# A second DMA queue and a new work order for the first quarter of a local-attention and feed-forward kernel

## The chip, the cores and the metric

The kernel runs on one core of one Trainium2 chip. The metric is device time of one execution in microseconds, the median of several runs. Everything is float32 in memory; each product is made of three matmuls of float32 halves, as told below.

## What is computed

```python
def reference(A_x, A_wqkv, A_wo, B_w1, B_w2):        # x 1x2048x640, wqkv 640x1920, wo 640x640, w1 640x1536, w2 1536x640
    xn = layernorm(A_x)
    q, k, v = heads(xn @ A_wqkv)                     # 32 heads of 20
    logits = q . k at positions s, s-2, ..., s-14    # 8 positions, dilation 2, masked below 0
    s = (softmax(logits * 20 ** -0.5) . v) @ A_wo
    g = silu(silu(xn @ B_w1) @ B_w2)
    return A_x + s * g
```

## The kernel before

The 2048 tokens are four groups of 512, and a group is four tiles of 128 tokens. For each group the kernel makes qkv in four quarters of the heads (`qkv_phase`), then the output projection of the group before, then the feed-forward part. A weight is cut into units of 128 rows: a unit is loaded raw, ScalarE copies it to its high half (L410), VectorE or GpSimd subtracts to get the low half (L413), and TensorE multiplies high by high, low by high and high by low. The transposed activations are split in the same way into `th` (high) and `tl` (low).

The order of the work isn't written out. Each operation is recorded with an engine, an estimated duration, what it reads and writes, and a priority; `Weave.order` then plays the program through with its own estimates and lines up, for each engine, whatever can start first. TensorE's operations alone keep the order in which they are recorded. So a changed priority or estimate moves instructions on ScalarE, VectorE, GpSimd and SyncE (SP, which issues DMAs) as far as the plan reaches.

The change is about the first quarter of group 0 (`first_quarter`), in which nothing has been loaded yet:

- `warm` (L625) fills TensorE with 22 transposes of the identity, `WARM`, before the first real work, and 3 more, `WARM2`, after the transposes of tile 0. Their results aren't used.
- SP issues x of tile 0 in two halves (L685), then the weight units and x of tiles 1 to 3 (L439), in the order of their priorities (`X_AT` for the x tiles). A weight unit is two DMAs: its q columns (L376, 96 KB) and its k and v columns (L377, 160 KB). In this text w0 to w4 are the five units of the first quarter, and x0 to x3 the four tiles.
- `begin(t)` is tile t's layernorm: `bn_stats` (L639), `bn_aggr` (L640), a square root on ScalarE (L453), a reciprocal (L455) and the scaling (L644, in two parts for tile 0). `turn(t)` transposes the tile on TensorE (L654), copies the high half on ScalarE (L658) and subtracts the low half on VectorE (L662).
- `products` (L667) records the 60 matmuls of 128x512 (L676), 15 for each tile: tile by weight high, tile low by weight high, tile by weight low.
- The low halves of the first weights go to VectorE for the units in `ON_DVE`, to GpSimd for the others below `LO`.

Engines work their queues in order: an instruction that waits holds up all that stand behind it on its engine.

Of the kernel before, what the change touches and what calls it, by code (L numbers as in the profile page):

```python
# [14 lines left out]
P = 128  # L15
# [8 lines left out]
T = 4  # L24
# [7 lines left out]
WARM, WARM2 = 22, 3  # L32
# [7 lines left out]
X_AT = 2, 7, 8  # L40
TILE_AT = 1, 1.5, 2, 2.5
LOW_AT = 3
ON_DVE = (2, 3, 4)
# [18 lines left out]
class Weave:  # L62
# [11 lines left out]
    EARLY = 10.0, 0.6  # L74
# [63 lines left out]
    def order(self):  # L138
# [6 lines left out]
        lanes = {e: [0.0] * self.LANES for e in ("SP", "POOL")}  # L145
# [5 lines left out]
        while len(done) < len(self.ops):  # L151
# [31 lines left out]
            if o.nbytes:  # L183
                dma = max(dma, t + dur) + o.nbytes / self.RATE
# [28 lines left out]
def local_attention_silu_ffn(ctx: ExitStack, tc: tile.TileContext, x, wqkv, wo, w1, w2, out):  # L213
# [84 lines left out]
    def dma(fn, reads, writes, nbytes, prio, dur=0.45, late=0.0):  # L298
        add("SP", dur, fn, reads, writes, prio, nbytes=nbytes, late=late)
# [52 lines left out]
    def raw_load(k):  # L352
# [17 lines left out]
        if u[0] == "q":  # L370
# [3 lines left out]

            def go():
                nc.sync.dma_start(r[:, :w], all3[:, 0, q * BQ:q * BQ + w])  # L376
                nc.sync.dma_start(r[:, w:].rearrange("p (s m) -> p s m", s=2), all3[:, 1:, q * CQ:(q + 1) * CQ])  # L377
            dma(go, [], kr, n * P * 4, 1 + k if k < 2 * DC else clock[0] + 5, dur=0.9,
                late=0.2 * k if k < 2 * DC else 0.0)
# [9 lines left out]
    def w_load():  # L389
# [16 lines left out]
        if not k:  # L406
# [8 lines left out]
            due if pool_does else LOW_AT if k < LO else 50, lock=True)  # L415
# [22 lines left out]
    def load_x(g, t, n=1, prio=None):  # L438
        dma(lambda: nc.sync.dma_start(XIN[:, t:t + n], rows(xg, g)[:, t:t + n]), [],  # L439
            [("xin", u) for u in range(t, t + n)], n * P * D * 4, clock[0] if prio is None else prio,  # L440
            late=LATE if g else 0.4 * t)
# [179 lines left out]
    def first_quarter(i):  # L621
# [6 lines left out]
        pe(4.5, lambda: warm(WARM, ROT[0]), ["consts"], [("rot", 0)])  # L628
# [54 lines left out]
        for k in range(2):  # L683
            cs = slice(k * 320, (k + 1) * 320)
            dma(lambda cs=cs: nc.sync.dma_start(XIN[:, 0, cs], rows(xg, 0)[:, 0, cs]), [],  # L685
                [("xin", 0) if k else ("xin", 0, "a")], P * 320 * 4, 0)
# [13 lines left out]
        products(0, [(0, 0), (1, 0), (0, 1), (1, 1), (2, 0), (0, 2), (1, 2)])  # L700
        turn(1)
        products(0, [(2, 1), (0, 3), (1, 3), (2, 2)])
        products(1, [(0, 0), (0, 1), (0, 2)])
        products(0, [(0, 4), (1, 4)])
        products(1, [(0, 3), (0, 4)])
        products(0, [(2, 3), (2, 4)])
        products(1, passes(1, 2)[:-3])
        turn(2)
        products(1, passes(2)[-3:])
        products(2, passes(0, 1, 2)[:-3])  # L710
        turn(3)
        products(2, passes(2)[-3:])
        products(3, passes(0, 1, 2))
# [225 lines left out]
    act(1, lambda: nc.scalar.activation(SD[:, 1, 0:1], epst, AF.Sqrt), ["consts"], [("rs", 0)], 0, "sqrt")  # L939
# [39 lines left out]
```

## Time and profile before

| | us |
|---|---|
| median of 3 runs | 621.68 |
| the runs | 621.67 to 622.61 |
| the profiled execution, its own time | 621.44 |
| its span, first to last instruction | 619.7 |
| TensorE busy (matmul rows) | 614.2, 99% of the span |
| VectorE busy | 561.3, 91% |
| ScalarE busy | 309.5, 50% |
| GpSimd busy | 112.8, 18% |

The span is 1.74 us less than the execution's own time; that part lies around the instructions. In timelines the first number is the start in us from the span's start, the second the length, then engine, line, operation, what is written and read, and the count; a bracket tells how long the engine had been idle and who ended it. Matmuls overlap, so a row's length is more than its share of the pace: the pace is read from start to start. Rows with SPq are DMA issues.

### The profile page before, as it was taken

What the parts mean: (1) busy time and instruction counts of PE and PEld (TensorE: products, weight loads), DVE (VectorE), ACT (ScalarE), POOL (GpSimd) and SP (SyncE); (2) the same over time, 40 slices, a digit from 0 to 9 for tenths busy, and PEclk for the clock granted to TensorE, in tenths of its full rate; (3) what the DMA queues carried; (4) which work ended last, traced back from release to release, by engine and by line L of the source; (5) the groups of instructions that cost most, each with busy time, mean ns of one, the idle gap of its engine ahead of it and who ended that gap; (6) DMA issues with size and microseconds to landing.
All of it is one profiled execution on the core that took longest, in us unless ns stands there. A gap on an engine that the chain in (4) does not pass through costs nothing.

```text
span 619.7 us, 9092 instructions
## 1 busy us (share of the span) xinstructions
PE 614.2 (99%) x3357; PEld 555.3 (90%) x3357; DVE 561.3 (91%) x581; ACT 309.5 (50%) x651; POOL 112.8 (18%) x168
## 2 busy tenths in 40 slices
PE   8999999999999999999999999999999999999997
PEld 7889999998889999999888999999888999998997
DVE  6558999999989997999998999999979999899974
ACT  5435558937376213951944502583396316152750
POOL 4510000011101133111212233311121213311100
PEclk9999999999999999999999999999999999999999
DMA  8999999866999998764699999855579998956642
GB/s 248 343 287 324 354 345 391 356 236 186 304 322 348 328 356 259 238 195 139 203 242 251 340 333 304 276 176 163 169 202 278 251 334 277 316 179 202 206 124 103
DMA packets 65449, 162.45 MB, mean 262 GB/s; under 512 B 7053, under 2 KB 29165, under 8 KB 65405
## 3 DMA queue, kind: packets, MB, share of 16 engines
q0 software_dynamic: 20016, 82.58, 44.6%
q1 hardware_dynamic: 45389, 79.29, 40.6%
q8 instruction: 26, 0.43, 0.3%
q14 instruction: 18, 0.15, 0.1%
HBM read 109.55 MB, written 34.16 MB: 232 GB/s over the span
## 4 chain that ended last, share of the span: by engine, by line
PE 98%; SPq 1%; DMA 0%; DVE 0%; issue 0%
PE acc L766 22%; PE acc L768 15%; PE acc L737 10%; PE acc L739 10%; PE acc L738 10%; PE rot L883 9%; PE rot L884 9%; PE rot L882 9%; PE acc L676 2%; PE rot L768 1%; DMA pr<-in_A_wqkv_dram 0%; PE rot L766 0%; SPq L376 0%; PE acc L864 0%; SPq L377 0%; PE rot L654 0%
## 5 line engine op out<-in xcount | busy, mean ns | idle before, releaser
L739 PE MATMUL acc<-w,th 128*128 128x512 f32 (+1 forms) x300 | 112.4, 375 | 0.0
L738 PE MATMUL acc<-w,tl 128*128 128x512 f32 (+1 forms) x300 | 112.4, 375 | 0.0
L737 PE MATMUL acc<-w,th 128*128 128x512 f32 (+1 forms) x300 | 112.4, 375 | 0.0
L766 PE MATMUL acc<-w,sh 128*128 128x384 f32 x384 | 111.7, 334 | 0.0
L768 PE MATMUL acc<-w,sh 128*128 128x256 f32 x384 | 107.1, 279 | 0.0
L888 ACT ACTIVATE sh<-rot 128x512 fp32r<-128x512 f32 x48 | 28.6, 597 | 154.2 <-PE rot L884 154.2
L884 PE MATMUL rot<-th,w 128*128 128x512 f32 x240 | 93.8, 391 | 0.0
L883 PE MATMUL rot<-tl,w 128*128 128x512 f32 x240 | 93.8, 391 | 0.0
L882 PE MATMUL rot<-th,w 128*128 128x512 f32 x240 | 93.5, 389 | 0.0
L571 DVE TENSOR_TENSOR pr<-q,kv 128x2560 f32<-128x2560 f32 x32 | 90.2, 2819 | 1.2 <-DMA raw<-in_A_wqkv_dram 1.0
L609 DVE TENSOR_TENSOR pr<-e,kv 128x2560 f32<-128x2560 f32 x32 | 90.3, 2823 | 0.7
L574 DVE TENSOR_REDUCE l<-pr 128x128 f32<-128x2560 f32 x32 | 90.1, 2815 | 0.5
L614 DVE TENSOR_TENSOR pr<-pr 128x1280 f32<-128x1280 f32 x64 | 74.0, 1156 | 1.5
L402 POOL DMA_DIRECT2D w<-half_w x72 | 38.5, 534 | 190.1 <-PE acc L768 94.0
L766 PEld LDWEIGHTS acc<-w,sh 128*128 128x128 f32 x384 | 72.1, 188 | 1.1
L768 PEld LDWEIGHTS acc<-w,sh 128*128 128x128 f32 x384 | 72.2, 188 | 0.9
L402 POOL DMA_DIRECT2D w<-half_q x52 | 27.6, 531 | 238.8 <-PE rot L884 113.5
L737 PEld LDWEIGHTS acc<-w,th 128*128 128x128 f32 x300 | 56.3, 188 | 8.6
L739 PEld LDWEIGHTS acc<-w,th 128*128 128x128 f32 x300 | 56.3, 188 | 8.6
L738 PEld LDWEIGHTS acc<-w,tl 128*128 128x128 f32 x300 | 56.3, 188 | 8.6
L487 ACT ACTIVATE xin<-sf 32x256 f32<-32x256 f32 (+1 forms) x144 | 54.6, 379 | 9.7 <-DVE sf L514 8.0
L766 PE MATMUL acc<-w,sl 128*128 128x384 f32 x192 | 56.1, 332 | 0.0
(104 smaller groups left out, 1059.5 us busy)
## 6 DMA issues: line engine op xcount, KB each, us to landing
w<-half_w POOLq DMA_DIRECT2D x72, 640.0 KB, 6.1
w<-half_q POOLq DMA_DIRECT2D x39, 512.0 KB, 4.3
half_w<-w SPq DMA_DIRECT2D x24, 640.0 KB
w<-half_wo POOLq DMA_DIRECT2D x15, 640.0 KB, 5.6
kv<-kv SPq DMA_DIRECT2D x15, 560.0 KB
half_q<-w SPq DMA_DIRECT2D x15, 512.0 KB
kv<-kv SPq DMA_DIRECT2D x15, 420.0 KB
gate<-in_B_w_dram SPq DMA_DIRECT2D x16, 320.0 KB
```

The source lines that it names most:

```text
L571: dve(2560, lambda t=t: nc.vector.tensor_tensor(out=PR, in0=win(qq[:, t:t + 2, :], W, 0), in1=win(kv[:, 0, t:t + 2, :], W, CQ), op=OP.mult ...
L574: dve(2560, lambda t=t: nc.vector.tensor_reduce(out=l[:, t:t + 2].rearrange("p t w h -> p (t w h)"), in_=PR.rearrange("p t w (h d) -> p (t ...
L609: dve(2560, lambda t=t, v=v: nc.vector.tensor_tensor(out=PR.rearrange("p t w (h d) -> p t (w h) d", d=DH), in0=e[:, t:t + 2].rearrange("p ...
L614: dve(2 * k * CQ, lambda k=k: nc.vector.tensor_tensor(out=PR[:, :, 0:k, :], in0=PR[:, :, 0:k, :], in1=PR[:, :, k:2 * k, :], op=OP.add), [] ...
L737: nc.tensor.matmul(o, hi, wh, start=c == 0, stop=False)
L738: nc.tensor.matmul(o, lo, wh, start=False, stop=False)
L739: nc.tensor.matmul(o, hi, wl, start=False, stop=c == DC - 1)
L766: nc.tensor.matmul(a[t][0][:, :CA], st, w[:, :CA], start=first, stop=last)
L768: nc.tensor.matmul(b[t // 2][0][:, h * CB:(h + 1) * CB], st, w[:, CA:], start=first and h == 0, stop=last, skip_group_check=True)
L882: nc.tensor.matmul(h, wh[:, cs], TH[i][:, c, :], start=c == 0, stop=False)
L883: nc.tensor.matmul(h, wh[:, cs], TL[i][:, c, :], start=False, stop=False)
L884: nc.tensor.matmul(h, wl[:, cs], TH[i][:, c, :], start=False, stop=c == DC - 1)
```

## The change

It does the following in the first quarter.

- 18 dummy transposes in place of 22.
- The raw loads of units 1 and 3 (w1 and w3 below, `BY_ACT`) are issued by ScalarE's queue. They are recorded as reading a key that the first square root of 1 element writes, so the four issues stand behind the table load on ScalarE.
- Other priorities: `X_AT`, `TILE_AT` (layernorms) and `LOW_AT` (low halves, now one number for each unit), and another set `ON_DVE`.
- Another order of the 60 matmuls and the tiles' transposes on TensorE, as a string `FIRST`.
- Other constants in the planner's estimate of when early DMAs land.

```diff
-WARM, WARM2 = 22, 3
+WARM, WARM2 = 18, 3
-X_AT = 2, 7, 8
-TILE_AT = 1, 1.5, 2, 2.5
-LOW_AT = 3
-ON_DVE = (2, 3, 4)
+X_AT = 2, 4.5, 7
+BY_ACT = 1, 3
+TILE_AT = 1, 1.5, 2, 3
+LOW_AT = 1.2, 1.7, 1.9, 1.9, 2.6, 3
+ON_DVE = (1, 2, 3, 5, 6, 7)
+FIRST = """0h0 0x0 0h1 0x1 0w0 0h2 0x2 T1 0w1 0h3 0x3 1h012 0h4 0x4
+           1h34 0w2 0w34 1x01234 1w01 T2 1w234 2h01234 2x01234 2w01 T3 2w234 3h01234 3x01234 3w01234"""
...
-    EARLY = 10.0, 0.6
+    EARLY = 8.0, 0.1, 350e3
...
+            by, queue = ("ACT", nc.scalar) if k in BY_ACT else ("SP", nc.sync)
             def go():
-                nc.sync.dma_start(r[:, :w], all3[:, 0, q * BQ:q * BQ + w])
-                nc.sync.dma_start(r[:, w:].rearrange("p (s m) -> p s m", s=2), all3[:, 1:, q * CQ:(q + 1) * CQ])
+                queue.dma_start(r[:, :w], all3[:, 0, q * BQ:q * BQ + w])
+                queue.dma_start(r[:, w:].rearrange("p (s m) -> p s m", s=2), all3[:, 1:, q * CQ:(q + 1) * CQ])
...
-            due if pool_does else LOW_AT if k < LO else 50, lock=True)
+            due if pool_does else LOW_AT[min(k, DC)] if k < LO else 50, lock=True)
```

In `FIRST`, `0x2` is tile 0's low half by w2's high half, `h` is high by high, `w` high by low, and `T1` the transposes of tile 1. Line numbers of the changed kernel are a few higher than those before: L410 is L414, L453 is L457, L413 is L417, L376 and L377 are L381 and L382.

ScalarE, from the table load on (w_73 to w_77 are the high halves of w0 to w4, th is the activations' high half, the L453 rows are the square roots of the layernorms). Before:

```order
L939 ACT_TABLE_LOAD
L939 ACTIVATE sd<-epst 128x1
L453 ACTIVATE sd<-mv,epst 128x1
L410 ACTIVATE w_73<-pr 128x512
L658 ACTIVATE th_69<-rot_113 128x3x128
L658 ACTIVATE th_69<-rot_114 128x2x128
L410 ACTIVATE w_74<-pr 128x512
L453 ACTIVATE sd<-mv,epst 128x1
L410 ACTIVATE w_75<-pr 128x512
L410 ACTIVATE w_76<-pr 128x512
L658 ACTIVATE th_69<-rot_113 128x3x128
```

ScalarE in the changed kernel, from the four DMA issues on:

```order
L382 DMA pr<-in_A_wqkv_dram 128x2x160
L457 ACTIVATE sd<-mv,epst 128x1
L414 ACTIVATE w_73<-pr 128x512
L662 ACTIVATE th_69<-rot_113 128x3x128
L662 ACTIVATE th_69<-rot_114 128x2x128
L414 ACTIVATE w_75<-pr 128x512
L414 ACTIVATE w_74<-pr 128x512
L457 ACTIVATE sd<-mv,epst 128x1
L414 ACTIVATE w_76<-pr 128x512
L414 ACTIVATE w_77<-pr 128x512
L662 ACTIVATE th_69<-rot_113 128x3x128
```

The high half of w2 (w_75) now stands ahead of that of w1 (w_74), both stand ahead of tile 1's square root, and the high half of w4 (w_77) stands ahead of tile 1's th.

SP in the changed kernel, from x0 on, with the semaphores that an issue waits for (the eight DMAHW numbers are the completion semaphores of the DMAs issued before, given out in turn; pr of row 2 is w0, of rows 5 and 6 w2, of rows 8 and 9 w4):

```order
L689 DMA xin<-in_A_x_dram 128x320 x2
L381 DMA pr<-in_A_wqkv_dram 128x192
L382 DMA pr<-in_A_wqkv_dram 128x2x160
L443 DMA xin<-in_A_x_dram 128x640
L381 DMA pr<-in_A_wqkv_dram 128x192 [waits DMAHW0_49]
L382 DMA pr<-in_A_wqkv_dram 128x2x160 [waits DMAHW2_49]
L443 DMA xin<-in_A_x_dram 128x640 [waits DMAHW3_49]
L381 DMA pr<-in_A_wqkv_dram 128x192 [waits DMAHW4_49]
L382 DMA pr<-in_A_wqkv_dram 128x2x160 [waits DMAHW5_49]
L381 DMA raw<-in_A_wqkv_dram 128x192 [waits DMAHW6_49]
```

Before, SP's first seven DMAs after x0 waited for nothing and all ten weight DMAs were its own; now the two queues share the eight semaphores, w2's second part waits for w0's first part to land, and x2 for w0's second part.

TensorE in the changed kernel, the first matmuls (acc_107 is tile 0's bank, acc_108 tile 1's):

```order
L631 MATMUL rot_113<-ident 128x128 x18
L658 MATMUL rot_113<-ident,xin 128x128 x3
L658 MATMUL rot_114<-ident,xin 128x128 x2
L631 MATMUL acc_112<-ident 128x128 x3
L680 MATMUL acc_107<-w_73,th_69 128x512
L680 MATMUL acc_107<-w_73,tl_71 128x512
L680 MATMUL acc_107<-w_74,th_69 128x512
L680 MATMUL acc_107<-w_74,tl_71 128x512
L680 MATMUL acc_107<-w_73,th_69 128x512
L680 MATMUL acc_107<-w_75,th_69 128x512
L680 MATMUL acc_107<-w_75,tl_71 128x512
L658 MATMUL rot_113<-ident,xin 128x128 x3
```

The third matmul still takes w1's high half (w_74), as before; what changed ahead of tile 1's transposes is the number of dummies alone.

## Rows read from the trace of the kernel before

**Rows 1.** Busy time by windows, TensorE alone, from the second quarter to the end.
```profile
24.00:616.00 592.00, 592.00 (x3254) 1.00 0.86 262
```

**Rows 2.** The chain that ended last, its start: start us, us, what.
```profile
6.06 0.47 SPq L376
6.57 3.04 DMA pr<-in_A_wqkv_dram
9.64 0.74 PE acc L676 x2
```

**Rows 3.** The timeline of TensorE, 1 to 15 us.
```profile
5.27 1.06 PE L627 MATMUL rot<-ident 128*128 128x128 f32 x4
6.13 1.21 PE L654 MATMUL rot<-ident,xin 128*128 128x128 f32 x5
...
7.56 0.49 PE L676 MATMUL acc<-w,th 128*128 128x512 f32 x1
...
8.49 0.39 PE L676 MATMUL acc<-w,th 128*128 128x512 f32 x1
...
9.64 0.50 PE L676 MATMUL acc<-w,th 128*128 128x512 f32 x1 [0.31 <-DMA pr<-in_A_wqkv_dram]
...
10.22 0.71 PE L654 MATMUL rot<-ident,xin 128*128 128x128 f32 x5
...
13.76 1.30 PE L676 MATMUL acc<-w,tl 128*128 128x512 f32 x5
14.90 0.61 PE L676 MATMUL acc<-w,th 128*128 128x512 f32 x2
```

**Rows 4.** The timeline of ScalarE, 0 to 12 us.
```profile
2.04 0.20 ACT L939 ACTIVATE sd<-epst 128x1 f32<-128x1 f32 x1
4.35 0.30 ACT L453 ACTIVATE sd<-mv,epst 128x1 f32<-128x1 f32 x1 [2.10 <-DVE mv L640]
5.65 0.63 ACT L410 ACTIVATE w<-pr 128x512 fp32r<-128x512 f32 x1 [1.00 <-DMA pr<-in_A_wqkv_dram]
7.01 0.76 ACT L658 ACTIVATE th<-rot 128x384 fp32r<-128x384 f32 x2 [0.73 <-PE rot L654]
7.66 0.63 ACT L410 ACTIVATE w<-pr 128x512 fp32r<-128x512 f32 x1
8.77 0.29 ACT L453 ACTIVATE sd<-mv,epst 128x1 f32<-128x1 f32 x1 [0.48 <-DVE mv L640]
8.97 1.14 ACT L410 ACTIVATE w<-pr 128x512 fp32r<-128x512 f32 x2
```

**Rows 5.** The timeline of VectorE, 3 to 12 us.
```profile
3.08 0.99 DVE L639 BATCH_NORM_STATS2 st<-xin 128x6 f32<-128x320 f32 x2 [1.63 <-DMA xin<-in_A_x_dram]
...
4.88 0.80 DVE L644 TENSOR_SCALAR xin<-xin,mv,sd 128x384 f32<-128x384 f32 x2
6.41 0.49 DVE L639 BATCH_NORM_STATS2 st<-xin 128x6 f32<-128x320 f32 x1 [0.73 <-DMA xin<-in_A_x_dram]
7.54 0.56 DVE L662 TENSOR_TENSOR tl<-rot,th 128x384 fp32r<-128x384 f32 x1 [0.63 <-ACT th L658]
...
9.30 0.71 DVE L644 TENSOR_SCALAR xin<-xin,mv,sd 128x640 f32<-128x640 f32 x1
```

**Rows 6.** Busy time by windows: PE, PEld, DVE, ACT, POOL busy; PEclk, DMA share, GB/s.
```profile
3.00:4.50 1.50, 1.50 (x9) 1.50 (x8) 1.20 (x3) 0.15 (x1) 0.22 (x1) 1.00 0.61 159
4.50:5.65 1.15, 1.15 (x7) 1.15 (x6) 0.93 (x3) 0.15 (x2) 0.00 (x0) 1.00 0.99 356
7.66:9.64 1.98, 1.57 (x6) 0.79 (x5) 1.84 (x6) 1.50 (x5) 1.27 (x1) 1.00 0.92 250
0.00:6.41 6.41, 5.03 (x24) 5.03 (x25) 2.57 (x16) 2.41 (x4) 2.65 (x8) 1.00 0.59 188
0.00:7.66 7.66, 6.28 (x31) 6.15 (x31) 3.19 (x17) 3.06 (x6) 3.89 (x8) 1.00 0.65 200
```

**Rows 7.** The timeline of SP's DMA issues: that of w2's second part.
```profile
4.59 0.43 SPq L377 DMA_DIRECT2D pr<-in_A_wqkv_dram  x1
```

## What the change should do to the time

> **What bounds the kernel now.** I read the views in this order. First busy time by windows: from 24 us to 616 us TensorE is busy for 592.00 of 592.00 us [rows 1]. The reader is to see that nothing in that stretch can be gained or lost by moving other engines' work a little; only what TensorE does before it runs without a break counts. Second the chain that ended last: it leaves the DMA issues of SP at 6.57, goes through a transfer of a weight and reaches TensorE at 9.64; from there it is TensorE alone [rows 2]. Third TensorE's own timeline: real matmuls start at 7.56, in pieces with idle time between, and from 9.64 they follow each other [rows 3]. By 9.64 five of the 60 matmuls of the first quarter have been done: two start at 7.56 and 8.15 or so, three from 8.49. So the time is **the moment from which TensorE runs without a break, less what it has done by then**, plus a fixed rest. A matmul's pace is (14.90 - 13.76) / 5 = 0.23 us [rows 3].
>
> What ended the wait at 9.64? The row names a DMA, but ScalarE shows more: it starts two weight copies at 8.97, the first of them (w2's high half, half of 1.14 us) ends at 9.54, and TensorE takes it at 9.64. ScalarE had stood idle before, then run the square root of tile 1 at 8.77 [rows 4]. So w2 had landed by 8.97 at the latest, and ScalarE's order had a share in the delay.
>
> **The change part by part.**
>
> *Four dummies fewer.* The last four dummies begin at 5.27 and the transposes of tile 0 at 6.13 [rows 3]: the place comes free 0.86 us earlier. The scaling of tile 0 begins at 4.88 and its two parts take 0.80 us [rows 5], 384 columns ready by about 5.37, the rest at 5.68. So the transposes begin at about 5.4, some 0.7 us earlier, the casts to th at 6.3 in place of 7.01 [rows 4], and the first matmul at about 7.1 in place of 7.56. This is on the path only if what follows is ready too.
>
> *Tile 0's low half.* VectorE now has both bn_stats of tile 1 ahead of it, not one. Tile 1 landed at 6.41 and two bn_stats take 0.99 us, so 7.4, then 0.56 us for the subtraction [rows 5]: 7.96, against 8.10 before. Second matmul at 8.0.
>
> *Four issues on ScalarE.* ScalarE is free at 2.24 and has to take the square root of tile 0 at 4.35 [rows 4]. The trace has no DMA issue on ScalarE; the nearest row is SP's, 0.43 us [rows 7], so four end at about 4.0 and cost nothing. If one took more than 0.53 us the square root would come later; tile 0's first matmuls have 1.5 us to spare (below), so the bound above is still nothing on the path unless an issue takes 0.9 us.
>
> *When the weights land.* From 3.0 to 4.5 the DMA engines are busy for a share of 0.61 and move 159 GB/s, from 4.5 on for 0.99 [rows 6]. So earlier issues can recover at most what was idle: 0.39 x 1.5 = 0.59 us; ScalarE's first transfer, issued at 2.24 and with about a microsecond from issue to data as an estimate, can fill some 0.47 of it. What is behind it is the same bytes through full engines. Bytes also say how far a landing lags behind the moving: by 6.41 the engines had moved 188 x 6.41 = 1.21 MB, and tile 1 landed then, which with all issued ahead of it is 0.92 MB: a lag of 0.29 MB [rows 6]. In the changed kernel w1 and w3 run on one queue beside x1, w2 and x2 on the other. And the two queues share eight completion semaphores: SP may issue w2's second part only when w0's first part has landed, before 5.65 by the copy of w0 [rows 4], while it was issued at 4.59 before [rows 7]. So w2 no longer comes well ahead of w3: it lands when x0, w0, x1, w1, w2 (1.44 MB) and between none and all of w3 (to 1.70 MB) have. With the lag this is 1.73 to 1.99 MB moved. Before, 200 x 7.66 = 1.53 MB had been moved by 7.66, and 250 GB/s were moved after it [rows 6]: 8.46 to 9.50, less the 0.47 recovered: 8.0 to 9.0. I take **8.2**, near the early end, since the engines were not quite full in that stretch (0.92) and two queues leave them less idle.
>
> A rule speaks against this part. The Trainium skill ("DMA: Bandwidth & Descriptors", on issuing engines not being separate DMA queues) says that transfers issued by several engines run on the same 16 DMA engines and interleave, and that only the sequencer's issue time is saved. The trace's share of 0.99 from 4.5 us agrees; what the rule would make of the sum if issue time were all that counts is the fifth rival's mechanism below.
>
> *ScalarE's order.* This is the term that decides. The third matmul needs w1's high half, and ScalarE now makes w2's first. However early w1 lands, its copy waits for w2: 8.2, a copy of 0.63, a copy of 0.63 [rows 4], with 0.1 us for the hops: **w1's high half is ready at 9.55**, against a third matmul at 8.49 before [rows 3]. Behind it stands tile 1's square root: 0.29, then reciprocal and scaling (0.71 by its row [rows 5]), so tile 1 can be transposed some 1.25 us after w1's half. TensorE does five matmuls meanwhile, 5 x 0.23 = 1.15: level within 0.1 us. I add 0.05 for it. The low half of w1 on VectorE follows under the transposes (0.71 again for five of them [rows 3]).
>
> *The rest of the order* (low halves on VectorE in place of GpSimd, T2 and T3 one or two matmuls later) lies beside TensorE's unbroken run. I cost it at nothing; its cover is that weights 3 and 4 land before TensorE asks for them at about 11.7 and 13.0.
>
> **The sum.** TensorE runs without a break from 9.55 with two matmuls done, before from 9.64 with five: 9.55 - 9.64 + 3 x 0.23 + 0.05 = **+0.65 us**. With w2 at 8.0 or 9.0 it is +0.45 or +1.45. On the profiled execution's 621.44 this gives 622.1. The median of the runs shown is 621.68, 0.24 above that execution, so on it **622.3**. About 0.2% (1.24 us) is what a measurement can tell, so the forecast is no change, on the slow side.
>
> **The rivals.**
>
> 1. *The weights land early and the new flow works.* If w2 lands by 7.0 to 7.5 (the DMA engines gain from two queues more than the idle share says), w1's half is ready at 8.35 to 8.85: -0.55 to -0.05 with the same sum; if ScalarE has both even before th, TensorE could start its third matmul right at 8.2: -0.7. For it: the windows show idle DMA engines ahead of 4.5. Against: only 0.59 us of it. Time 621.0 to 621.6, I say 621.3.
>
> 2. *w4 becomes the wait, the slower side.* ScalarE's copy of w4 now stands ahead of tile 1's th, before it stood behind. TensorE asks for tile 1's th at about 12.1; the copy (0.63) and the first cast (0.4) must fit ahead of it, so w4 must land by 11.0. In the trace the copy of w4 comes later than 10.11, where w3's ends [rows 4], and x2 now runs ahead of w4. From 11.0 every microsecond adds one to the +0.65: landing at 11.8 gives 623.7 on the median's basis with w2 as forecast, less if TensorE had waited before anyhow. For it: x2's 0.33 MB at 250 GB/s is 1.3 us. Against: w4's issue has not moved back.
>
> 3. *The clock.* Five transposes took 1.21 us at 6.13 and 0.71 at 10.22 [rows 3]: the array went from the lower of its two levels (1.2 GHz) to the higher (2.4 GHz) between, after TensorE had worked without a break. With four dummies fewer and idle time between 7.4 and 9.55 it may come up later or fall again; each matmul at the lower level costs another 0.2 us, five of them 1.0: 623.3. The Trainium skill ("TensorE: Matmul & The Clock Gate", Part 1) has the slow level as the default and activity as what releases it, which speaks against fewer dummies; the rows of tile 0 and tile 1 agree with it. Against: dummies and transposes still fill the time up to 7.1.
>
> 4. *ScalarE's issues are dear*, 0.9 us or more each, and tile 0 waits for its square root. Then the whole start moves by what lies over 0.9: 623 or so. Nothing in the trace speaks for it. That the issues don't start early at all belongs here: the four stand behind the table load, and if the shared semaphores hold them or SP, the change does nothing for the transfers and the order alone is left.
>
> 5. *Issue time was the bound.* The chain shows SP's issues one after another up to 6.57 [rows 2]. Four issues less are 4 x 0.43 = 1.7 us; with all of it TensorE would run from 7.1 with nothing done: 7.1 - 9.64 + 5 x 0.23 = -1.39, 620.3. Against: the busy share [rows 6].
>
> **How the numbers follow.** The forecast has 0.52, rival 1 has 0.24, rival 2 0.10, rival 3 0.06, rival 4 0.04, rival 5 0.04. Faster by over 0.2% is rival 5: 0.04. Slower by over 0.2% (over 622.9) is rivals 2 to 4 for the most part, 0.11 of their 0.20 since each begins small, and the late end of the forecast, 0.04: 0.15. The rest, 0.81, is within. The range takes the forecast with both bounds of w2's landing (622.1 to 623.1), rival 1 from 621.0 on, and the smaller part of rivals 2 and 3: 620.9 to 623.5.
>
> **What would show it.** Right: ScalarE idle until w2 lands near 8.2 with w1 already there, its copies back to back, TensorE's third matmul at about 9.5, its first at about 7.1. Right on transfers: a DMA share near 1 from 3.5 us on. Wrong: a third matmul before 8.7, or another idle stretch of TensorE after it (rival 2 at about 12, rival 3 in longer transposes at tile 1). A total under 621 would mean that the sum mis-sized w2's landing.

## The result and the profile after

| | before | after |
|---|---|---|
| median of 13 runs each, us | 621.43 | 624.46 |
| lowest and highest | 621.11, 623.21 | 622.35, 627.91 |
| the profiled execution, its own time and span | 621.44, 619.7 | 627.91, 626.1 |

The ratio is 1.0048 with a 95% interval of 1.0032 to 1.0064: **3.0 us slower**, where +0.65 was forecast, and outside the range. The profiled execution is the slowest of the 13, so it shows more than the median does.

TensorE's idle time in it, by who ended it (the view of waits; us in total, times, the longest):

```profile
PE acc L762 <- ACT sh L884: 2.6, 1, 2.6
PE rot L631 <- POOL ident masks.py:199: 1.4, 1, 1.4
PE acc L680 <- ACT th L662: 0.7, 1, 0.7
PE acc L680 <- DVE tl L666: 0.6, 1, 0.6
PE rot L658 <- DVE xin L648: 0.5, 1, 0.5
PE acc L680 <- ACT w L414: 0.4, 1, 0.4
```

The 1.4 is the wait for the identity that all kernels here have. Four waits lie in the first 10 us, and the longest is elsewhere, at the first product of the feed-forward part. Start first, TensorE's timeline:

```profile
5.98 0.77 PE L658 MATMUL rot<-ident,xin 128*128 128x128 f32 x5 [0.51 <-DVE xin L648]
6.59 0.49 PE L631 MATMUL acc<-ident 128*128 128x128 f32 x3
7.76 0.50 PE L680 MATMUL acc<-w,th 128*128 128x512 f32 x1 [0.68 <-ACT th L662]
8.87 0.70 PE L680 MATMUL acc<-w,tl 128*128 128x512 f32 x1 [0.60 <-DVE tl L666]
9.97 0.79 PE L680 MATMUL acc<-w,th 128*128 128x512 f32 x1 [0.40 <-ACT w L414]
10.56 0.63 PE L680 MATMUL acc<-w,tl 128*128 128x512 f32 x1
10.99 1.05 PE L680 MATMUL acc<-w,th 128*128 128x512 f32 x2
```

Matmuls begin at 7.76, 8.87 and 9.97; before at 7.56, about 8.15 and 8.49 [rows 3]. From 9.97 on TensorE isn't idle, but the pace is wrong: 10.99 - 10.56 = 0.43 us for a matmul that takes 0.23 [rows 3]. The windows of this kernel say why (columns as in [rows 6]):

```profile
7.66:9.64 1.98, 1.21 (x2) 0.39 (x2) 1.76 (x6) 1.19 (x4) 1.03 (x1) 0.84 0.86 246
9.64:11.40 1.76, 1.43 (x3) 1.16 (x4) 1.71 (x4) 1.33 (x4) 0.00 (x0) 0.50 0.90 256
12.40:14.90 2.50, 2.50 (x15) 2.16 (x14) 1.63 (x6) 1.85 (x4) 0.90 (x1) 1.00 1.04 316
28.00:623.00 595.00, 591.89 (x3245) 536.47 (x3243) 547.03 (x535) 296.29 (x619) 103.59 (x155) 1.00 0.85 259
73.84:77.26 3.42, 3.42 (x15) 3.42 (x14) 3.42 (x4) 2.09 (x4) 0.00 (x0) 0.50 1.05 384
```

The granted clock falls to 0.50, the lower level (1.2 GHz), from 8.99 to 12.40, after three pieces of idle time of 0.51, 0.68 and 0.60 us that end at 5.98, 7.76 and 8.87, with five transposes, three dummies and one matmul between them. It does so again from 73.84 to 77.26, after the long wait. And the row that stood for an unbroken run before ([rows 1], 592.00 of 592.00) is now 591.89 of 595.00. The clock column shows no low value before the first rise, though there is one: in the trace of the kernel before, dummies and tile 0's transposes begin 0.21 us apart until 7.17 us and 0.11 us apart from there on, while [rows 6] read 1.00 throughout. In d0 below, which is the same kernel, the pace changes at 4.21 us. So the moment of the first rise differs from execution to execution.

ScalarE, timeline of the start (ACTq is its queue of DMA issues):

```profile
0.75 1.28 ACT L935 ACT_TABLE_LOAD   x1 [0.75 <-PEq L961]
0.92 0.38 ACTq L381 DMA_DIRECT2D pr<-in_A_wqkv_dram  x1
1.34 0.44 ACTq L382 DMA_DIRECT2D pr<-in_A_wqkv_dram  x1
1.81 0.49 ACTq L381 DMA_DIRECT2D pr<-in_A_wqkv_dram  x1
2.04 0.20 ACT L935 ACTIVATE sd<-epst 128x1 f32<-128x1 f32 x1
4.15 0.39 ACTq L382 DMA_DIRECT2D pr<-in_A_wqkv_dram  x1
4.92 0.29 ACT L457 ACTIVATE sd<-mv,epst 128x1 f32<-128x1 f32 x1 [2.67 <-DVE mv L644]
6.70 0.63 ACT L414 ACTIVATE w<-pr 128x512 fp32r<-128x512 f32 x1 [1.49 <-DMA pr<-in_A_wqkv_dram]
7.24 0.74 ACT L662 ACTIVATE th<-rot 128x384 fp32r<-128x384 f32 x2
8.77 1.15 ACT L414 ACTIVATE w<-pr 128x512 fp32r<-128x512 f32 x2 [0.79 <-DMA pr<-in_A_wqkv_dram]
```

Three issues run beside the table load, though they stand behind it in the order; w1 thus goes out ahead of w0 and x1. The fourth begins at 4.15, when x0's second half is there. Tile 0's square root is at 4.92 (4.35 before), w0's copy at 6.70 (5.65) [rows 4]. At 8.77 stand w2's copy and then w1's, as forecast; but TensorE idles only 0.40 us for them, since the second matmul is late itself. VectorE shows what the x tiles lost by it:

```profile
4.15 0.49 DVE L643 BATCH_NORM_STATS2 st<-xin 128x6 f32<-128x320 f32 x1 [0.26 <-DMA xin<-in_A_x_dram]
...
7.47 0.89 DVE L643 BATCH_NORM_STATS2 st<-xin 128x6 f32<-128x320 f32 x2 [1.22 <-DMA xin<-in_A_x_dram]
8.27 0.54 DVE L666 TENSOR_TENSOR tl<-rot,th 128x384 fp32r<-128x384 f32 x1
```

Tile 0's second half and all of tile 1 are awaited; tile 1's statistics begin at 7.47, not 6.41, and tile 0's low half stands behind both of them [rows 5].

The wait at 70 us. ScalarE before, then after (L888 and L884 are the Silu, the copies of 128x640 are units of the feed-forward weights):

```profile
63.34 0.80 ACT L410 ACTIVATE w<-gate 128x640 fp32r<-128x640 f32 x1
64.15 1.28 ACT L888 ACT_TABLE_LOAD   x1
65.45 0.60 ACT L888 ACTIVATE sh<-rot 128x512 fp32r<-128x512 f32 x1
65.94 0.59 ACT L889 ACTIVATE sf<-rot 128x512 f32<-128x512 f32 x1
66.42 0.74 ACT L410 ACTIVATE w<-gate 128x640 fp32r<-128x640 f32 x1
```

```profile
67.28 0.80 ACT L414 ACTIVATE w<-gate 128x640 fp32r<-128x640 f32 x1
70.63 0.74 ACT L414 ACTIVATE w<-gate 128x640 fp32r<-128x640 f32 x1 [2.56 <-issue]
71.39 1.28 ACT L884 ACT_TABLE_LOAD   x1
72.68 0.60 ACT L884 ACTIVATE sh<-rot 128x512 fp32r<-128x512 f32 x1
```

The planner has put one more copy ahead of the table load and the first Silu. ScalarE stands at it for 2.56 us (the view names no releaser: "issue"), and TensorE, which needs the Silu, for 2.58. Nothing that the diff touches by name is here: the plan of the first 24 us differs, and the planner's choices 45 us later differ with it.

### The profile page after: what moved, and what is told of

It reads as the page before. It is cut to its first block, busy times and chain, and to the rows that moved or that the text cites. A ratio compares the mean times of both kernels' runs of the same rounds, so it can differ in the third digit from the quotient of the medians.

```text
span 626.1 us, 9083 instructions
## 1 busy us (share of the span) xinstructions
PE 616.3 (98%) x3353; PEld 556.2 (89%) x3353; DVE 564.1 (90%) x584; ACT 310.7 (50%) x652; POOL 111.3 (18%) x165
## 4 chain that ended last, share of the span: by engine, by line
PE 89%; DMA 6%; SPq 2%; issue 1%; ACT 1%; DVE 1%; ACTq 0%; DVEq 0%
PE acc L762 22%; PE acc L764 15%; PE rot L879 8%; PE rot L880 8%; PE rot L878 8%; PE acc L735 8%; PE acc L733 8%; PE acc L734 8%; DMA half_q<-w 2%; DMA kv<-kv 2%; DMA pr<-in_A_wqkv_dram 1%; DMA raw<-in_A_wqkv_dram 1%; DMA gate<-in_B_w_dram 1%; PE acc L680 1%; SPq L381 1%
## 5 line engine op out<-in xcount | busy, mean ns | idle before, releaser
L762 PE MATMUL acc<-w,sh 128*128 128x384 f32 x384 | 113.1, 337 | 2.6 <-ACT sh L884 2.6
L884 ACT ACTIVATE sh<-rot 128x512 fp32r<-128x512 f32 x48 | 28.7, 597 | 144.2 <-PE rot L880 133.0
L762 PEld LDWEIGHTS acc<-w,sh 128*128 128x128 f32 x384 | 73.0, 190 | 3.9 <-ACT sh L884 3.0
L618 DVE TENSOR_TENSOR pr<-pr 128x1280 f32<-128x1280 f32 x64 | 75.3, 1177 | 1.2
L764 PEld LDWEIGHTS acc<-w,sh 128*128 128x128 f32 x384 | 73.1, 190 | 0.9
```

The lines of the kernel that those rows point to most:

```text
L618: dve(2 * k * CQ, lambda k=k: nc.vector.tensor_tensor(out=PR[:, :, 0:k, :], in0=PR[:, :, 0:k, :], in1=PR[:, :, k:2 * k, :], op=OP.add), [] ...
L762: nc.tensor.matmul(a[t][0][:, :CA], st, w[:, :CA], start=first, stop=last)
L764: nc.tensor.matmul(b[t // 2][0][:, h * CB:(h + 1) * CB], st, w[:, CA:], start=first and h == 0, stop=last, skip_group_check=True)
```

## The experiments

All kernels at a glance. The 60th matmul is the last of the first quarter; "rest" is from its start to the end of TensorE's work, both in the profiled execution. "Low" counts timed runs whose mean granted clock was 0.998 or less (the stretch from 73.84 to 77.26 at half takes 3.42 x 0.5 / 626 = 0.003 off it; for the kernel before all its runs beside the experiments are counted). The ratio is to the kernel before on the same chip, whose medians lay between 621.43 and 622.29; 0.001 is 0.62 us. The profiled execution is the slowest of its kernel's runs for the change, d2, e2 and g4, and the fastest for g5 and g7, so the first three columns are one execution each and not the median.

| kernel | third matmul | 60th | rest | low | ratio and interval |
|---|---|---|---|---|---|
| before | 8.49 | 23.91 | 592.10 | 2 of 146 | |
| d0 before again | 8.22 | 23.68 | 593.62 | 0 of 1 | a single run |
| d3 18 dummies alone | 8.22 | 23.66 | 592.83 | 0 of 11 | 0.9996 (0.9979 to 1.0014) |
| d2 second queue alone | 9.04 | 24.45 | 594.37 | 0 of 12 | 1.0001 (0.9988 to 1.0013) |
| g4 ScalarE's order alone | 9.73 | 26.50 | 592.10 | 2 of 11 | 1.0020 (1.0010 to 1.0029) |
| f2 later order alone | 8.52 | 23.93 | 593.27 | 2 of 12 | 1.0015 (0.9995 to 1.0036) |
| g7 start, one queue, ScalarE as before | 8.29 | 24.61 | 592.10 | 1 of 12 | 1.0016 (1.0000 to 1.0031) |
| g6 start, ScalarE and VectorE as before | 8.74 | 24.63 | 592.11 | 1 of 12 | 1.0013 (1.0000 to 1.0027) |
| g2 start, ScalarE as before | 8.97 | 25.27 | 592.51 | 1 of 11 | 1.0020 (1.0010 to 1.0029) |
| g5 g2, two low halves later | 9.44 | 25.88 | 592.10 | 2 of 8 | 1.0030 (1.0013 to 1.0046) |
| f1 the whole start | 10.46 | 26.90 | 592.11 | 9 of 12 | 1.0031 (1.0015 to 1.0046) |
| f3 f1 and fill | 9.90 | 25.87 | 592.39 | 0 of 12 | 1.0020 (1.0006 to 1.0034) |
| f4 f3, w1 first | 10.29 | 26.00 | 592.11 | 0 of 12 | 1.0022 (1.0008 to 1.0036) |
| the change | 9.97 | 25.89 | 596.58 | 7 of 13 | 1.0048 (1.0032 to 1.0064) |
| e0 the change again | 9.72 | 26.15 | 593.30 | 8 of 12 | 1.0027 (1.0013 to 1.0041) |
| e1 issues on SP | 9.46 | 24.73 | 593.37 | 3 of 11 | 1.0015 (1.0003 to 1.0027) |
| e2 fill | 9.86 | 24.67 | 597.31 | 2 of 12 | 1.0031 (1.0015 to 1.0048) |
| e3 a copy behind the Silu | 9.94 | 24.81 | 594.59 | 7 of 12 | 1.0023 (1.0009 to 1.0037) |
| d1 w1 first | 9.06 | 24.60 | 596.70 | 3 of 12 | 1.0033 (1.0019 to 1.0047) |

**The change again, and the kernel before again.** No edit.

> The changed kernel once more, unaltered, as the run that the next three are held against. The profile of its slowest run shows three losses: the third matmul at 9.97 us (before 8.49), TensorE at its lower clock level from 8.99 to 12.40, and a stall of 2.6 us at 70.4 behind a weight copy on ScalarE that stands ahead of the first Silu, with a second stretch at the lower level after it. If these are what the median of +3.0 is made of, this run shows the first in full and the others in some executions: 622 to 626, 624.5 as the middle.

> The kernel before once more, for a second profile: first to tell whether its later part has stalls too on another chip. Theory S (the later loss is the change's own, made by the shifted plan): the 60th matmul of the first quarter at about 23.9 us and TensorE's rest from there 592.1 us, without stalls over 0.3 us. Theory R (the later stalls come and go with the transfers in any version): a rest of 593 us or more.

Measured: the change 624.49 (12 runs), the kernel before 622.74 in its single run. The size of the loss differs between the two measurements of the change (intervals 1.0032 to 1.0064 and 1.0013 to 1.0041), its sign doesn't. The kernel before, too, has executions with a wait near 73 us (0.99 in d0; 0.47 and 1.45 in d3 and d2 below, which keep its plan), so its rest isn't always 592.1.

**The parts alone.** 18 dummies, and the second queue, each in the kernel before.

```diff
-WARM, WARM2 = 22, 3
+WARM, WARM2 = 18, 3
```

> The kernel before with 18 dummies in place of 22 and nothing else changed: tile 0 is transposed 0.7 us earlier, the first matmul about 0.5 earlier; the third waits for w1's copy as before, now with a longer gap. Without a drop of the clock the same time as before within 0.3 us; if four dummies are what keeps the clock, a granted clock under 0.999 in some executions and 1 to 2 us more in those.

```diff
+                queue = nc.scalar if k in (1, 3) else nc.sync
-                nc.sync.dma_start(r[:, :w], all3[:, 0, q * BQ:q * BQ + w])
+                queue.dma_start(r[:, :w], all3[:, 0, q * BQ:q * BQ + w])
```

> The kernel before with w1 and w3 issued by ScalarE's queue and nothing else changed: 22 dummies, its own order on every engine. If the issues beside the table load delay x0's second half and w0, tile 0's square root is at 4.9 in place of 4.35, the first matmul 0.4 to 1 us later, but w1's copy no longer waits and the third matmul follows the second; the unbroken run starts at about 9.5 to 10. If the queue alone made the change slow, this is 1 us or more slower than before; if the orders did, it is within 0.5 us of before.

Neither costs anything that can be measured over all, and neither brings anything; a loss of up to 0.8 us by the queue lies within its interval. No run of either shows the lower clock. The queue does move the start: in d2 tile 1's statistics begin at 7.70, the first matmul at 7.99, the 60th 0.5 to 0.8 us later than in the three profiles without it (before, d0, d3). The Trainium skill ("DMA: Bandwidth & Descriptors", on issuing engines not being separate DMA queues) has the transfers of several issuing engines run on the same 16 DMA engines and interleave. The ratio of d2, 1.0001, agrees: nothing was gained, and only the order of the transfers changed.

**The issues back on SP**, at the change's places in the plan:

```diff
-            by, queue = ("ACT", nc.scalar) if k in BY_ACT else ("SP", nc.sync)
+            by, queue = ("ACT", nc.sync) if k in BY_ACT else ("SP", nc.sync)
```

> The changed kernel with w1 and w3 issued by SP at the places that the plan gives them; every other order as in the change. Theory A (the two queues are the cause at the start: the issues on ScalarE begin at 0.92 us, beside the table load, and put w1 and half of w3 ahead of the second half of x0 and of w0): tile 0's square root goes back from 4.92 to about 4.35, w0's copy from 6.70 to about 5.7, the third matmul to 9.0 or earlier, and the time falls by 1 us or more against the change. Theory B (ScalarE's order, w2's copy ahead of w1's, is the cause): tile 0 is back to its times, but the third matmul stays at 9.3 to 9.7 and the time is within 0.5 us of the change less what the clock gives. The stall at 70 may stay under both, since the plan of that stretch is the same.

Measured: the first two matmuls at 6.97 and 7.57, earlier than before, so x0 and x1 were late by the queue. The third comes at 9.46, 1.39 us of idle time behind ScalarE's copy, and the ratio is still 1.0015; the median is 0.8 us below e0's. w1 also goes out later on SP here, so this run doesn't separate the order of copies from w1's landing; g4 below does.

**Dummies in the gaps:**

```diff
-        pe(0.11 * WARM2, lambda: warm(WARM2, ACC[5]), [], [("acc", 5)])
+        pe(0.11 * WARM2, lambda: warm(9, ACC[5]), [], [("acc", 5)])
...
+            if step in ("0h0", "0x0"):
+                pe(0.0, lambda: warm(8, ACC[5]), [], [("acc", 5)])
```

> The changed kernel with 22 more dummy transposes on TensorE in the gaps of the start: 9 in place of 3 after tile 0's transposes, 8 after the first matmul and 8 after the second. The plan of the other engines is unchanged. If the lower clock level from 8.99 to 12.40 came from the idle time before it, the granted clock stays at the higher level there, five matmuls and the transposes of tile 1 take 0.23 us and 0.71 us again in place of 0.43 and 0.78, and the time falls by about 1.1 us in the executions that had the drop, 0.5 to 1 in the median. If the drop has nothing to do with idle time, no change. The stall at 70 stays.

Measured: no fall of the clock at the start, the 60th matmul at 24.67 against 25.89 and 26.15 with it. But in this execution, the slowest of the 12, TensorE is then early at 70 us and waits there: the median is not better.

```profile
PE acc L764 <- ACT sh L886: 2.5, 1, 2.5
...
PE rot L658 <- DVE xin L648: 0.7, 1, 0.7
```

**The copy of the seventh feed-forward unit behind the first Silus** (the planner's list, that copy and what needs it moved):

```diff
+        x, after = self.copy[26], self.silu[0]
...
+        for o in done[:a] + rest + late + done[b + 1:]:
```

> The changed kernel with one instruction group moved: the high-half copy of the seventh feed-forward weight unit, which stands ahead of the first Silu on ScalarE, comes after the two Silus of that step, as it did before the change (its subtraction and store follow it). If the wait of that copy for its weight's transfer is what stalls TensorE at 70 us, the stall goes, and with it the stretch at the lower level after it: up to 4 us in the slowest executions, 0.5 to 2 in the median; the start is as in the change. If the stall is caused by the transfers themselves, it reappears a step later and the time stays.

Measured: the first Silu is no longer late (68.36), but the next copy waits 1.73 us for a DMA (by the view, the store of an earlier unit's half) and the second Silu stands behind it: TensorE waits 1.4 us there. So the copy's place was only a part of it. The rest points at the transfers, but isn't shown: SP issues two of these units at 61.64 here and at 57.76 in the kernel before, yet at 59.77 to 61.32 in d0, d3 and d2 as well, where the first Silu isn't late.

**w1's copy ahead of w2's on ScalarE:**

```diff
+        done.remove(self.copy[1])
+        done.insert(done.index(self.copy[2]), self.copy[1])
```

> The changed kernel with one instruction moved: on ScalarE the copy of w1 stands ahead of that of w2. In all profiles of the change w1 has landed by 4.7 us and w2 at 8.4 to 8.7. If ScalarE's order is the wait at the third matmul, it starts right after the second, at 8.5 to 9.1 in place of 9.7 to 9.97, TensorE has three more matmuls done when w2's half is there, the 60th matmul comes 0.5 to 0.9 us earlier, the gaps are shorter so that the clock drops in fewer executions, and the median falls by 0.5 to 1.5 us. If something else also holds the third matmul, no change.

Measured: third matmul 0.33 us behind the second, as before, but the second is at 8.73, tile 1's transposes wait (0.39), and the 60th comes at 24.60: no earlier than with fill (24.67), and 0.2 us earlier than in e3, whose clock doesn't fall at the start either (24.81). Expected were 0.5 to 0.9 us. So in the change itself the order of these two copies decides little. At the first Silu it waits 2.3 us and the clock falls behind that (72.20).

**Start and later order apart.** In f1 everything that the kernel before does behind its first quarter's last matmul is done in that kernel's order, on all engines; f2 is the mirror.

```diff
-        for o in self.order():
+        rest = set(TAIL)
+        for o in [o for o in done if o.seq not in rest] + [by[s] for s in TAIL]:
```

> The start of the change (dummies, the two queues, all orders of the first quarter), and from the last matmul of the first quarter on every engine in the order of the kernel before. Theory 1 (three parts: the start costs 0.9 us, the clock drop after its gaps another 1.3 in about half of the executions, and the new order later a wait for the first Silu of up to 2.9): the first down matmul comes at 69.5 to 71.0 with less than 0.6 us of idle time ahead of it, the waits of 0.2 to 0.5 near 227, 378 and 393 us are gone, so that 526.8 us are left after the fifth feed-forward unit begins; the median lies 0.3 to 1.7 us above before, and some executions still show the lower clock. Theory 2 (the start alone): as the change itself, 1.7 to 3.0 us above before. Theory 3 (the later order alone): as before, within 0.3 us.

> The mirror: the start of the kernel before, and from the last matmul of its first quarter on every engine in the order of the change. Theory 1: the last matmul of the first quarter as before (23.7 to 23.9), no lower clock at the start; the copy of the seventh feed-forward unit stands ahead of the first Silu and TensorE waits 2 to 3 us at about 69 us, with the first down matmul at 71 to 72.5; the lower clock may follow that wait; the median lies 1.0 to 2.5 us above before. Theory 2 (the start alone): as before, within 0.3 us. Theory 3 (the later order alone): 1.7 to 3.0 us above before.

Measured: f1 is 624.06 against 621.86, with the clock low in 9 of 12 runs. So the start alone makes most of the loss, more than expected; its rest is 592.11, as before. Its profile has the latest tile 1 of all (statistics at 7.96) and so the latest 60th matmul. f2 starts as before and waits at the first Silu, less than expected and with an interval that takes in no loss:

```profile
69.84 0.44 PE L833 MATMUL acc<-w,sh 128*128 128x384 f32 x1 [1.05 <-ACT sh L955]
```

**The whole start with fill, and with w1 first besides.** Edits as in e2 and d1, on f1.

> The first of these kernels with 22 further dummy transposes in the gaps of the start (9 in place of 3 behind tile 0, 8 behind its first matmul, 8 behind its first low matmul). Theory 1: no execution shows the lower clock, and what is left is the start without it: the last matmul of the first quarter at 24.5 to 24.9, the median 0 to 0.9 us above before (less than 0.9 where before waits at the first Silu itself). If the gaps have nothing to do with the clock, the lower clock comes as often as without the dummies.

> That kernel with the copy of w1 ahead of that of w2 on ScalarE as well. Theory 1: the third matmul begins within 0.4 us of the second, as before, but tile 1's transposes then wait for their layernorm; the last matmul of the first quarter at 24.3 to 24.7, the median within 0.6 us of before, and not below it, since tile 0's late second half (ScalarE's issues ahead of it in the queues) is still there. If ScalarE's order were the whole of the loss at the start, the last matmul of the first quarter would come at 23.9 or earlier.

Measured: no run of the 24 shows the lower clock, against 9 of 12 without the dummies. So the gaps of the start are what lets the clock fall. Yet the median improves by 0.5 us only, and the 60th matmul comes at 25.87 and 26.00, later than expected: another wait appears at tile 2's transposes that the slow stretch had hidden (0.96 us in f3, 0.70 in f4). f3's ScalarE, VectorE, GpSimd and TensorE:

```profile
14.83 0.63 ACT L482 ACTIVATE w<-raw 128x512 fp32r<-128x512 f32 x1 [1.02 <-DMA raw<-in_A_wqkv_dram]
15.37 0.28 ACT L525 ACTIVATE sd<-mv,epst 128x1 f32<-128x1 f32 x1
```

```profile
15.88 1.47 DVE L716 TENSOR_SCALAR xin<-xin,mv,sd 128x640 f32<-128x640 f32 x1
```

```profile
13.13 6.12 POOL L809 MEMSET kv<- 2x2240 f32 x3
```

```profile
17.41 0.77 PE L726 MATMUL rot<-ident,xin 128*128 128x128 f32 x5 [0.96 <-DVE xin L716]
```

VectorE in e2, where these transposes don't wait:

```profile
15.46 0.61 DVE L648 TENSOR_SCALAR xin<-xin,mv,sd 128x640 f32<-128x640 f32 x1
```

Tile 2's square root stands behind a copy whose unit hasn't landed; before, the root came first. But e2 has that order too, and its root is only 0.42 us earlier (14.95). The greater part is the scaling: 1.47 us in f3, 2.10 in f4 and 2.11 in f1, against 0.61 in e2. It runs beside GpSimd's three memsets of 2x2240, which begin at 13 to 14 us in these three kernels, at 24.77 in the kernel before and at 26.04 in e2. So most of this wait comes of joining the two orders and not of the change. The medians of f3 and f4 can hold 0.7 to 0.9 us of it; without it the start with fill would cost 0.8 to 1.0 us. That is an estimate from these rows: 623.54 less 0.86 (1.47 - 0.61) or 0.70, against 621.86. In f4 the third matmul stands right behind the last dummies at 10.29, so the fill had become the wait, and w1's place isn't tested by it.

**ScalarE's order alone**, in the kernel before: HEAD is the change's list of ScalarE's first 29 operations without the issues.

```diff
+        first = [by[s] for s in HEAD]
+        q[:len(first)] = first
```

> The kernel before (22 dummies, one queue, its own orders everywhere), and on ScalarE alone, in the first quarter, the order of the change: w2's copy ahead of w1's, w4's ahead of tile 1's th, the seventh unit's ahead of tile 2's square root. If ScalarE's order makes the loss at the start: the third matmul begins 1 us or more behind the second and at 9.4 or later, tile 2's transposes wait, the lower clock shows in part of the executions, the last matmul of the first quarter comes at 24.6 or later, and the median lies 0.7 to 2 us above before. If the loss needs ScalarE's queue or the other engines' orders: the last matmul of the first quarter by 24.1 and the median within 0.5 us of before.

ScalarE, TensorE and a window of g4:

```profile
8.54 1.15 ACT L429 ACTIVATE w<-pr 128x512 fp32r<-128x512 f32 x2 [1.30 <-DMA pr<-in_A_wqkv_dram]
```

```profile
7.02 0.50 PE L695 MATMUL acc<-w,th 128*128 128x512 f32 x1 [0.55 <-ACT th L677]
7.73 0.50 PE L695 MATMUL acc<-w,tl 128*128 128x512 f32 x1 [0.22 <-DVE tl L681]
9.73 0.50 PE L695 MATMUL acc<-w,th 128*128 128x512 f32 x1 [1.50 <-ACT w L429]
```

```profile
11.46:13.44 1.98, 1.98 (x7) 1.79 (x8) 1.66 (x4) 1.04 (x3) 0.00 (x0) 0.50 0.99 337
```

This is the forecast's mechanism by itself: TensorE idle for 1.50 us at the third matmul, then the lower clock in this execution, and 1.0020. It doesn't need the clock: the 9 of its 11 runs without a fall have a median of 622.87, 1.4 us above before. No other part alone has an interval that lies clear of 1.

**The start without ScalarE's order**, the later order as before: g2 has only ScalarE's list of before; g5 also puts two low halves on VectorE behind the tiles' scaling; g6 has ScalarE's and VectorE's lists of before; g7 has VectorE's order of the change, but one queue. The early memsets lengthen the scaling of tiles 2 and 3 in these four as well (0.71 to 1.31 us), but no wait of TensorE over 0.25 us follows from it in their profiles.

```diff
+        for low, scale in LATER:
+            q.insert(q.index(by[scale]) + 1, by[low])
```

> The change with ScalarE's order of before in the first quarter (the four issues stay on ScalarE ahead of it) and every engine's order of before behind it; VectorE, GpSimd, SP, TensorE and the dummies of the first quarter as in the change. If ScalarE's order makes the loss at the start: third matmul within 0.5 us of the second, last matmul of the first quarter at 24.5 or earlier, no lower clock, median within 0.5 us of before. If VectorE's order has its own share: tile 1's transposes still wait, since the low half of w2 stands ahead of tile 1's reciprocal and scaling there and w2's copy now comes after w1's: a gap of 0.4 to 1 us ahead of them, and the last matmul of the first quarter at 24.6 to 25.2.

> The same, and on VectorE the low half of w2 behind tile 1's scaling and that of the sixth unit behind tile 2's. What is left of the change at the start: 18 dummies, the second queue, the order of TensorE and the other low halves. If the copies and low halves that stand ahead of tile work make the loss: tile 1's transposes wait less than 0.3 us, no lower clock, last matmul of the first quarter at 24.0 to 24.5 and the median within 0.4 us of before. If the second queue with its late second half of x0 makes it: the first matmul at 7.6 or later and the last of the first quarter still at 24.6 or later, the median 0.8 us or more above before.

> The change's dummies, second queue, order of TensorE and choice of low halves for VectorE; ScalarE's and VectorE's orders at the start as before (tile 0's low half ahead of the second bn_stats of tile 1, tile 1's scaling ahead of the low halves of the weights), and all engines as before behind the first quarter. If the orders of these two engines are the loss: the second matmul within 0.8 us of the first, tile 1's transposes without a wait over 0.3 us, last matmul of the first quarter at 24.2 to 24.6, no lower clock, median within 0.5 us of before. If the second queue by itself, through the later x0, x1 and w0, is the loss: last matmul at 24.9 or later and the median 0.8 us or more above before.

> The change's dummies, choice and order of low halves on VectorE and GpSimd, and order of TensorE; all ten weight loads on SP in the order of before, ScalarE's order at the start as before, all engines as before behind the first quarter. If VectorE's order hurts only where x1 lands late (second queue): x1's bn_stats begin by 6.6 as before, the second matmul comes within 0.9 us of the first, the last of the first quarter by 24.4, and the median within 0.5 us of before. If VectorE's order hurts by itself: tile 1's transposes wait 0.5 us or more, last matmul at 24.5 or later, median 0.7 us or more above before.

g7's VectorE and TensorE show VectorE's share, with tile 1 in time:

```profile
6.56 0.89 DVE L728 BATCH_NORM_STATS2 st<-xin 128x6 f32<-128x320 f32 x2 [0.90 <-DMA xin<-in_A_x_dram]
7.36 0.54 DVE L751 TENSOR_TENSOR tl<-rot,th 128x384 fp32r<-128x384 f32 x1
...
8.90 0.69 DVE L502 TENSOR_TENSOR w<-pr,w 128x512 fp32r<-128x512 f32 x1 [0.60 <-ACT w L499]
```

```profile
7.96 0.50 PE L765 MATMUL acc<-w,tl 128*128 128x512 f32 x1 [0.59 <-DVE tl L751]
...
10.37 0.77 PE L743 MATMUL rot<-ident,xin 128*128 128x128 f32 x5 [0.72 <-DVE xin L733]
```

w2's low half stands ahead of tile 1's scaling and waits for w2: 0.72 us at the transposes. g6 waits only 0.28 there; its second matmul is late for the later x1 (statistics at 7.39). Both reach the 60th matmul at 24.6, 0.7 to 0.95 us behind before, and both intervals reach down to 1.0000. So each of the queue and VectorE's order delays the start; together (g2) they make 25.27, with a ratio clear of 1. g5 was expected to be better than g2 and was worse. In its profile the clock falls at 8.40, though its gaps (0.61, 0.72, 0.61) are much like g2's (0.81, 0.55, 0.64), where it didn't. That doesn't explain the ratio: the six runs of g5 without a fall took 623.47 to 624.27, no less than the two with one (623.41 and 623.58), and no profile shows one of the six. Why the clock falls in one kernel and not in the other stays open too. One thing that differs is the moment of the first rise, by the pace of the dummies 4.42 us in g2 and about 5.0 in g5; no run tests whether that decides.

## Why the prediction was wrong

- **Forecast and its mechanism.** ScalarE makes w2's half ahead of w1's and the third matmul waits: right, and g4 shows it alone. Forecast for it were w2 at 8.2 and the third matmul at 9.55; in the change 8.77 and 9.97, in g4 8.54 and 9.73. The landing of w2 was inside its bounds of 8.0 to 9.0. The sum, too, was near for the start without a fall of the clock: +0.65 forecast, 0.9 to 1.1 in e3 (60th matmul at 24.81 against 23.68 and 23.91). That is partly luck, since the first two matmuls were forecast for 7.1 and 8.0 and came at 7.71 and 8.82 there, and "the term that decides" did not decide (d1). What failed is what the sum put at nothing: the issues on ScalarE, the clock, and the rest of the order.
- **"Four end at about 4.0 and cost nothing"** failed first. The issues began at 0.92, not at 2.24. w1 went ahead of w0 and x1, tile 1 came 1.06 us later (7.47), w0's copy 1.05 later. d2 puts this at 0.5 to 0.8 us of the start. The step had taken tile 1's landing over from before, unchanged.
- **Dummies and tile 0's low half.** Second matmul forecast for 8.0: it is at 7.96 in g7, where there is one queue, and at 8.87 in the change. The two bn_stats ahead of the low half were counted rightly; the date of tile 1 wasn't. The transposes of tile 0, forecast for 5.4, are at 5.39 in g7 and at 5.98 in the change: the place was free, but the late x0 held them.
- **The clock**, rival 3 with a chance of 0.06, is what happened in 7 of 13 and 8 of 12 runs. These runs have medians of 625.35 and 625.00, the others 623.63 and 622.96: falls, at the start or later, go with 1.7 and 2.0 us more. The price of one at the start was about right (1.0 forecast; 25.89 and 26.15 against 24.60 to 24.81 without a fall are 1.1 to 1.5); the chance wasn't. The forecast itself had TensorE idle for most of the time from 7.6 to 9.55, with two matmuls in it; so the clock belonged inside the forecast, not beside it. Fill shows it (f3 and f4: none of 24, f1: 9 of 12). The Trainium skill ("TensorE: Matmul & The Clock Gate", Part 1) has the slow level as the default and activity as what releases it; the window of the change at 0.50 (9.64 to 11.40), behind the gaps, agrees.
- **"The rest of the order ... I cost it at nothing"** failed twice: VectorE's w2 ahead of tile 1's scaling (0.72 in g7), and the copy ahead of the first Silu (2.58 in the change, 1.05 in f2). The first hides behind ScalarE's order, which is why taking that away gave so little (d1); the second varies between executions (none in e0, 2.5 in e2). The copy ahead of tile 2's root, a third such place, makes no wait in the change.
- **"Nothing in that stretch can be gained or lost by moving other engines' work a little"** was true of the one execution in [rows 1], not of every execution of that kernel (d0 idles 0.99 us near 73 us), and not of a new plan. The rest of TensorE's work took 592.10 to 592.51 in all but three profiles with the later order of before (592.83 to 594.37 in those) and 593.27 to 597.31 in the seven with the change's.
- **Rivals 1, 2, 4 and 5.** w2 did not land early; no wait of TensorE for tile 1's th shows in the change, so w4 was no wait; issues took 0.38 to 0.49 each, as SP's; and with four issues fewer on SP nothing was gained (d2), so issue time was not the bound.

The sum: with the later order of the change, the start costs 0.7 to 1.2 us without the clock's fall and 2.0 to 2.5 with it (60th matmul 24.60 to 24.81 and 25.89 to 26.15, before 23.66 to 23.91; 26.90 in f1), and the later order up to 2.6 more and another fall. What is not settled: the exact share of the later order in the median (f2's interval takes in 1), what the copy at 70 us waits for, and what decides about a fall among nearly equal gaps. No kernel tried was faster than the one before.

## What to carry to other kernels

Where a planner lays out the order, a changed constant at the start is a changed plan everywhere: compare the order of every in-order engine along the whole kernel, and look for a copy that has to wait and has come to stand ahead of work that TensorE needs. Price the granted clock with every gap that the forecast itself opens. Taking one wait away shows the next, so find the share of each by putting single parts into the old kernel, not only by taking them out of the new one. A kernel joined from two orders can have waits that neither has (f3): look for them before its time is read as the share of a part.

## What was not expected of the hardware

- DMA issues that stand behind a table load on ScalarE ran beside it: the load from 0.75 to 2.03, the issues from 0.92.
- After gaps of 0.51, 0.68 and 0.60 us between pieces of TensorE's work the granted clock fell to 0.50 (from 8.99 to 12.40), in some executions and not in others of the same kernel (7 of 13 runs show a fall, there or later).
- A second queue gained nothing over all (d2: 1.0001), but changed which transfer came first: w1 went out ahead of w0, and tile 1 came later (its statistics begin at 6.89 to 7.96 in the profiles with the queue, at 6.17 to 6.72 in those without).
- VectorE's scaling of a tile (128x640) took 0.61 to 0.62 us in the 39 cases in the first quarters of all profiles where it began beside no long GpSimd instruction. The 18 that began while GpSimd made a low half or a memset ended 0.35 us after the end of that instruction, whenever they began, and took 0.65 to 2.11 us. The 0.71 of [rows 5] is one of these.
